# Block 0's softmax with one exponential of 256 columns for a unit, and the maximum and the sums on VectorE

## The chip, the cores and the metric

The kernel runs on one core of a Trainium2 chip. The metric is the device time of one execution in microseconds (us). Three runs of the kernel before took 833.86, 834.26 and 834.46 us; their median is 834.26 us. The times below come from one profiled execution, and "us" counts from the start of its span.

## The reference

Three layers follow one another, all in float32. The first is attention in chunks: for each of 2 x 8 heads, a chunk of 32 queries looks at 8 memory keys and at 56 keys around it (fewer at the two ends of the sequence).

```python
scores = scale * np.matmul(q_c, k_full.transpose(0, 1, 3, 2))
scores = scores - np.max(scores, axis=-1, keepdims=True)
a = np.exp(scores)
a = a / (np.sum(a, axis=-1, keepdims=True) + 1e-09)
out[:, :, c_start:c_end] = np.matmul(a, v_full)
...
h = x @ w_in
g = (a[0] + a[1] * h + a[2] * h2 + a[3] * h3) / (1.0 + abs(b[0]) * abs(h) + abs(b[1]) * h2 + 1e-6)
x = g @ w_out
...
for e in range(4):
    out += p[:, e : e + 1] * (np.maximum(x @ w1[e], 0.0) @ w2[e])
```

The 1536 tokens have 512 features; the second layer has 2048 hidden features, each of the four experts of the third has 1024.

## The kernel before, in words

**Tiling.** The tokens form three blocks of 512. The attention of a block is cut into 8 units: a pair of heads (4 pairs) by one half of the block (256 tokens). Units 0 to 7 are block 0, 8 to 15 block 1, 16 to 23 block 2. A unit has one tile `w` of SBUF (named `T` in the code) with its keys, values, queries and then its probabilities, one small tile `st` with 4 columns of maxima and 4 of sums, and one PSUM bank each for scores, transposed probabilities and values (tags `att` and `acc`). A row of the scores tile holds 4 softmaxes of 64 columns, 256 columns together.

**One unit, step by step** (`Unit.parts`). In block 0 the keys come compact and are spread out (`spread_k`, 448 columns, and `spread_m`, 64 columns; line 284 on VectorE, 283 on ScalarE, 492 on GpSimd). TensorE makes the scores (`scores`, line 433, with the mask of line 430 at an end of the sequence). VectorE takes the negated maximum of each 64 columns (`peaks`, line 439), GpSimd scales it (`peaks2`, line 445), ScalarE takes four exponentials of 64 columns with the maximum as bias and the sum as by-product (`exps`, line 449; the trace shows each as an ACTIVATE and an accumulator read). GpSimd adds 1e-9 to the sums (`norm1`, 455), VectorE takes the reciprocal (`norm2`, 458), GpSimd multiplies (`norm3`, 462). TensorE transposes (`trans`, 468), two copies of 64 partitions bring the result to SBUF (`probs`, 284 or 283), and TensorE makes the values (`values`, 485). ScalarE and VectorE split them into a high and a low part of the tile `x` (lines 557 and 562): TensorE works on three products of such parts for each float32 product.

**The second layer.** A step takes 128 hidden features of one block: 12 matmuls of the first product (`first_ops`, line 606), a chain of some ten operations on ScalarE, VectorE and GpSimd for the quotient, and 12 matmuls of the second product (`second_ops`, line 718). The weights arrive as 64-bit words. VectorE turns them into float32 in three steps (`conv1` to `conv3`, lines 354, 360 and 366, tile `y`), then ScalarE takes the high part (line 283, `w<-y`) and GpSimd the low one (line 328). The first step of block 0 starts as soon as units 0 to 7 and the first weight are there. The units of block 1 are worked on between the steps of block 0, those of block 2 between the steps of block 1. The third layer (from about 340 us) has matmuls at lines 606, 832 and 965.

**What sets the order.** The program lists all operations with their engines and planned costs (`add`). `Plan.run` then places them one by one: on each engine the operation that can start first, earliest due time first; where an operation has several ways (spreading copies, the copies of block 0's probabilities, low parts), the engine on which it would end first. It gives the order of each queue, the engine of such operations, the order of SP's loads and the number of filling matmuls (line 296) in planned gaps of TensorE at the start. GpSimd's operations, and those of VectorE added with `lock=True`, are planned one after the other, never side by side:

```python
if e == "POOL" or e == "DVE" and o.lock:
    t = max(t, lock)
```

On the chip each engine works its queue in that order and waits at its head for what the instruction needs. The planned costs of one unit's softmax stand in `parts` from line 529 on.

Of the kernel before, what the change touches and what calls it, by code (L numbers as in the profile page):

```python
# [16 lines left out]
AF = mybir.ActivationFunctionType  # L17
ALU = mybir.AluOpType
AX = mybir.AxisListType
# [6 lines left out]
KB = KW + NM  # L26
NQ = 4
# [5 lines left out]
UB = BLK // UT * KT  # L33
# [6 lines left out]
SCALE = float(D) ** -0.5  # L40
# [7 lines left out]
FU = 11  # L48
RU = 12
PAD = 192 // 4  # L50
FGAP = 0.5
LAG = 3
GS = 4, 4, 8
# [34 lines left out]
class Op:  # L88
# [6 lines left out]
    def at(self, e):  # L95
        return max((a.start + 0.5 if a.eng == e == "SP" else a.end + Plan.lag(a.eng, e) for a in self.after), default=0.0)


class Plan:
# [7 lines left out]
    def add(self, ways, fn, after=(), uses=(), takes=(), key=None, lock=False):  # L107
        op = Op(len(self.ops), ways, fn, key)
        op.lock = lock
        self.ops.append(op)  # L110
        for a in after:
            if a is not None:
                op.after.append(a)
                a.next.append(op)
        op.takes = list(takes)
        op.bufs = list(takes) + list(uses)
        for b in op.bufs:
            b.users.append(op)
        return op
# [134 lines left out]
def emit(ctx: ExitStack, tc: tile.TileContext, qk, v0, kv, q8, w64, w32, coef, prob, out):  # L254
# [3 lines left out]
    PE, ACT, DVE, POOL, SP = nc.tensor, nc.scalar, nc.vector, nc.gpsimd, nc.sync  # L258
    engines = {"ACT": ACT, "DVE": DVE, "POOL": POOL}
    plan = Plan()  # L260
    add = plan.add

    def sb(shape, dt, tag, name=None):
        return pool.tile(shape, dt, tag=tag, bufs=BUFS.get(tag, 1), name=name or tag)
# [4 lines left out]
    def make(b):  # L269
        p = psum if b.tag in ("acc", "h", "att") else pool  # L270
        b.ap = p.tile(b.shape, b.dt, tag=b.tag, bufs=BUFS[b.tag], name=b.tag)
# [123 lines left out]
    class Unit:  # L395
# [11 lines left out]
        def parts(self):  # L407


            u, blk, hp = self.u, self.blk, self.hp  # L410
            self.at = {}
            at = lambda part_, n: self.at[part_][0].ap[:, self.at[part_][1] : self.at[part_][1] + n]
            p1, p2, p3 = lambda: at(0, UT), lambda: at(1, UT), lambda: at(2, UT)


            T = Buf("w", [128, 2048], F32)
            st = Buf("st", [128, 8], F32)
            wide = lambda j: slice(j * 64, j * 64 + 64)
            k = lambda j: T.ap[:, wide(j)]
            q = lambda j: T.ap[:, 1024 + j * 64 : 1024 + j * 64 + 64]  # L420
            s = lambda: T.ap[:, : NQ * KB]
            v = lambda: T.ap[:, 512:1024]
            nm, sm = lambda: st.ap[:, 0:4], lambda: st.ap[:, 4:8]
# [27 lines left out]
                        bias=nm()[:, n : n + 1], accum_out=sm()[:, n : n + 1],  # L451
                    )

            def norm1():
                POOL.tensor_scalar(out=sm(), in0=sm(), scalar1=1e-9, scalar2=None, op0=ALU.add)

            def norm2():
                DVE.reciprocal(out=sm(), in_=sm())
# [64 lines left out]
            else:  # L523
# [3 lines left out]
            o1 = yield 0, scores, [*ready, o_mask, o_ident], [T]  # L527
            P1 = self.at[0][0]
            o = add([("DVE", 0.33)], peaks, [o1], [P1], [st])
            o = add([("POOL", 0.15)], peaks2, [o], [st])  # L530
            o = add([("ACT", 1.16)], exps, [o], [P1, st, T])
            o = add([("POOL", 0.15)], norm1, [o], [st])
            o = add([("DVE", 0.09)], norm2, [o], [st])
            o = add(
                [("POOL", 0.65)], norm3, [o], [st, T]
            )
# [16 lines left out]
            if first:  # L553
# [9 lines left out]
                    out=X.ap[:, 1, c], in0=ps(), in1=X.ap[:, 0, c].bitcast(F32), op=ALU.subtract  # L563
# [5 lines left out]
    def cost_of(parts):  # L569
        return PARTS[parts[0]] if len(parts) == 1 else SWITCH + sum(GROUPED[n] for n in parts)  # L570
# [534 lines left out]
    o = add([("SP", 0.1)], load_probs, [steps[nA - 1].firsts[0]])  # L1105
# [35 lines left out]
    for a, b in zip(pe, pe[1:]):  # L1141
        if a.n == last:
            break
        n = int((b.start - a.end - FGAP) / MM)
        if n > 0:
            fill[a] = min(n, 16)
    with tc.manual_schedule():
        ACT.preload_act_table_set("natural_log_exp_and_others")

        make(next(b for o in listed for b in o.takes if b.tag == "st"))  # L1150
        sb([128, PAD], F32, "pad")
        for o in listed:
# [82 lines left out]
```

## Time and profile before

| | |
|---|---|
| median of 3 runs | 834.26 us |
| the profiled execution | 835.54 us |
| its span, first to last instruction | 833.4 us |
| TensorE busy (matmul) | 816.5 us, 98% |
| VectorE busy | 613.8 us, 74% |
| GpSimd busy | 381.3 us, 46% |
| ScalarE busy | 361.9 us, 43% |
| mean granted TensorE clock | 0.997 |
| bytes moved by DMA | 55.41 MB, of which 24.92 MB in the first 80 us |

The span is shorter than the time of its execution by 2.1 us, which lie before the first and behind the last instruction. A share of the whole span is a mean over stages that differ: the first 50 us hold 16 of the units and the first steps, and everything behind is mostly matmuls. The page names engines PE (TensorE), PEld (its weight loads), DVE (VectorE), ACT (ScalarE), POOL (GpSimd) and SP (the engine that issues the loads). Back-to-back instructions of VectorE and ScalarE overlap in the trace, so the distance between two starts says what a queue can do, and the duration how long a result takes.

### The profile page before, as it was taken

The numbers are of one execution on the slowest core, as the hardware profiler recorded it, in microseconds if no ns is written. First come the engines' busy times: TensorE is split into PE (matmuls) and PEld (weight loads), VectorE is DVE, ScalarE is ACT, GpSimd is POOL, SyncE is SP. The second block draws the span as 40 slices with busy tenths as digits, with TensorE's granted clock in tenths as the row PEclk, the third lists the DMA queues.
The fourth block names the chain that finished last, engine by engine and source line by source line (L and its number), as shares of the span: only waits on it lengthen the run. The fifth ranks groups of instructions, "written<-read, shape, count | busy, mean of one in ns | idle before, by whom it ended". The sixth has DMA issues, their size and how long they took to land.

```text
span 833.4 us, 11348 instructions
## 1 busy us (share of the span) xinstructions
PE 816.5 (98%) x4208; PEld 663.6 (80%) x4213; DVE 613.8 (74%) x913; ACT 361.9 (43%) x792; POOL 381.3 (46%) x349
## 2 busy tenths in 40 slices
PE   7899999999999999999999999999999999999998
PEld 4667787788777888888888888888888888888886
DVE  5988789999987689775765765765765765765754
ACT  6899887666777675330230230230230330330310
POOL 4896767787779699440330330330330330330300
PEclk9999999999999999999999999999999999999999
DMA  9985031122220101010100100100100100100003
GB/s 347 353 310 187 27 127 39 63 77 76 75 77 23 30 0 51 1 51 1 51 29 23 51 28 25 50 27 25 51 28 25 51 26 26 52 25 1 1 1 151
DMA packets 21910, 55.41 MB, mean 66 GB/s; under 512 B 3936, under 2 KB 3936, under 8 KB 21856
## 3 DMA queue, kind: packets, MB, share of 16 engines
q1 hardware_dynamic: 21856, 54.69, 19.0%
q8 instruction: 33, 0.54, 0.3%
q14 instruction: 21, 0.17, 0.1%
HBM read 51.54 MB, written 3.15 MB: 66 GB/s over the span
## 4 chain that ended last, share of the span: by engine, by line
PE 71%; DVE 14%; ACT 5%; DMA 3%; POOL 3%; issue 2%; SPq 1%; DVEq 0%; ACTq 0%; POOLq 0%
PE acc L965 31%; PE att L606 12%; PE h L832 10%; PE att L832 7%; PE acc L718 5%; PE h L606 4%; DVE ts L687 3%; DVE y L354 2%; DVE y L360 2%; DVE tm L679 2%; DVE tm L675 2%; POOL ts L706 1%; DMA w<-q 1%; DVE y L366 1%; DMA w<-kv 1%
## 5 line engine op out<-in xcount | busy, mean ns | idle before, releaser
L328 POOL TENSOR_TENSOR w<-stg,w 128x512 fp32r<-128x512 f32 x64 | 95.6, 1503 | 315.7 <-ACT w L283 315.7
L982 DVE SCALAR_TENSOR_TENSOR p<-acc,pr,p 128x512 f32<-128x512 f32 x180 | 135.1, 751 | 100.5 <-PE acc L965 100.5
L965 PE MATMUL acc<-w,g 128*128 128x512 f32 x768 | 176.7, 389 | 0.0
L965 PEld LDWEIGHTS acc<-w,g 128*128 128x128 f32 x768 | 144.1, 188 | 29.9
L606 PE MATMUL att<-x,w 128*128 128x512 f32 x624 | 147.6, 389 | 0.0
L718 PE MATMUL acc<-g,w 128*128 128x512 f32 x576 | 144.0, 394 | 1.8 <-ACT g L283 1.1
L606 PEld LDWEIGHTS att<-x,w 128*128 128x128 f32 x624 | 117.1, 188 | 24.3
L718 PEld LDWEIGHTS acc<-g,w 128*128 128x128 f32 x576 | 106.7, 188 | 28.4 <-DVE p L737 1.9
L283 ACT ACTIVATE ts<-h 128x512 f32<-128x512 f32 x15 | 9.0, 598 | 239.1 <-PE h L832 239.1
L606 PE MATMUL h<-x,w 128*128 128x512 f32 x384 | 97.4, 396 | 1.0 <-DVE ts L687 0.7
L965 PE MATMUL acc<-w,gb 128*128 128x512 f32 x384 | 89.6, 389 | 0.0
L965 PEld LDWEIGHTS acc<-w,gb 128*128 128x128 f32 x384 | 72.1, 188 | 15.0
L606 PEld LDWEIGHTS h<-x,w 128*128 128x128 f32 x384 | 70.4, 188 | 16.5 <-DVE ts L687 1.5
L328 POOL TENSOR_TENSOR g<-ts,g 128x512 fp32r<-128x512 f32 x48 | 69.6, 1452 | 12.2 <-ACT g L283 11.9
L706 POOL TENSOR_TENSOR ts<-ts,tu 128x512 f32<-128x512 f32 x48 | 65.7, 1370 | 10.9 <-ACT ts L695 7.2
L328 POOL TENSOR_TENSOR w<-y,w 128x512 fp32r<-128x512 f32 x35 | 45.5, 1303 | 18.6 <-ACT w L283 18.0
L832 PE MATMUL att<-x,w 128*128 128x512 f32 x180 | 45.7, 389 | 0.0
L832 PE MATMUL h<-w 128*128 128x512 f32 x180 | 45.7, 389 | 0.0
L832 PE MATMUL h<-x,w 128*128 128x512 f32 x180 | 45.7, 389 | 0.0
L283 ACT ACTIVATE g<-ts 128x512 fp32r<-128x512 f32 x48 | 30.2, 630 | 25.2 <-DVE ts L687 24.9
L283 ACT ACTIVATE w<-tu 128x512 fp32r<-128x512 f32 x30 | 19.0, 633 | 48.9 <-POOL tu L763 43.2
L832 PEld LDWEIGHTS h<-w 128*128 128x128 f32 x180 | 33.8, 188 | 7.0
(122 smaller groups left out, 1177.1 us busy)
## 6 DMA issues: line engine op xcount, KB each, us to landing
stg<-w SPq DMA_DIRECT2D x64, 512.0 KB, 3.6
w<-kv SPq DMA_DIRECT2D x32, 256.0 KB, 5.3
w<-q SPq DMA_DIRECT2D x16, 256.0 KB, 5.0
w<-qk SPq DMA_DIRECT2D x8, 400.0 KB, 6.6
out<-p SPq DMA_DIRECT2D x12, 256.0 KB, 2.0
w<-v SPq DMA_DIRECT2D x8, 256.0 KB, 6.3
pr<-prob SPq DMA_DIRECT2D x1, 24.0 KB, 3.8
cf<-coef SPq DMA_DIRECT2D x1, 3.0 KB, 5.8
```

The costliest lines, as they stand in the source:

```text
L283: return lambda o, i: ACT.activation(o, i, AF.Copy)
L328: engines[op.eng].tensor_tensor(out=dst[:, 1], in0=src, in1=dst[:, 0].bitcast(F32), op=ALU.subtract)
L354: DVE.tensor_scalar(out=y.ap, in0=words(1), scalar1=3, scalar2=0x3FFFFFF8, op0=ALU.logical_shift_left, op1=ALU.bitwise_and,)
L360: DVE.scalar_tensor_tensor(out=y.ap, in0=words(1), scalar=-(1 << 30), in1=y.ap, op0=ALU.bitwise_and, op1=ALU.bitwise_or,)
L606: PE.matmul(s.h.ap, wt[w].ap[:, 0, a, k * 128 : (k + 1) * 128], xs[k].ap[:, b], start=(k == 0 and n == 0), stop=(k == KT - 1 and n == 2),)
L675: [("DVE", 0.6)], lambda: DVE.tensor_tensor(out=m.ap, in0=m.ap, in1=h.ap, op=ALU.mult), [li], [h, m]
L687: lambda: DVE.scalar_tensor_tensor(out=out.ap, in0=in0.ap, scalar=scalar, in1=in1.ap, op0=op0, op1=op1),
L706: lambda: POOL.tensor_tensor(out=s.ap, in0=s.ap, in1=u.ap, op=ALU.mult), [ln], [s, u],
L718: PE.matmul(ps, wt[f].ap[:, 1, a, d * 128 : (d + 1) * 128], g.ap[:, b], start=start, stop=stop)
L832: PE.matmul(ps.ap, left(a, k), right(b, k), start=k == 0 and n == 0, stop=k == 1 and n == 2,)
L965: PE.matmul(ps.ap, gs[j][0].ap[:, a, d * 128 : d * 128 + 128], wt[f].ap[:, 1, b], start=j == 0 and n == 0, stop=j == 1 and n == 2,)
L982: DVE.scalar_tensor_tensor(out=y, in0=ps.ap, scalar=p, in1=y, op0=ALU.mult, op1=ALU.add)
```

## The change

For units 0 to 7 the softmax is written in another way; units 8 to 23 keep theirs. VectorE subtracts the maximum from the 256 columns of scores and writes them to the unit's tile in SBUF (`less`), ScalarE takes one exponential over these 256 columns in place, with the scale in it (`exp_all`), VectorE sums each 64 columns (`sums`), and the addition of 1e-9 goes to VectorE. The scaling of the maximum on GpSimd falls away. `less`, `sums` and the addition are added without a lock.

```diff
+SPLIT_EXP = lambda u: u < UB
...
-            def norm1():
-                POOL.tensor_scalar(out=sm(), in0=sm(), scalar1=1e-9, scalar2=None, op0=ALU.add)
+            def less():
+                e = s().rearrange("p (n k) -> p n k", n=NQ)
+                DVE.tensor_tensor(
+                    out=e, in0=p1().rearrange("p (n k) -> p n k", n=NQ),
+                    in1=nm().unsqueeze(2).to_broadcast([128, NQ, KB]), op=ALU.add,
+                )
+
+            def exp_all():
+                ACT.activation(s(), s(), AF.Exp, scale=SCALE)
+
+            def sums():
+                DVE.tensor_reduce(
+                    out=sm(), in_=s().rearrange("p (n k) -> p n k", n=NQ), axis=AX.X, op=ALU.add
+                )
+
+            def norm1(eng):
+                engines[eng].tensor_scalar(out=sm(), in0=sm(), scalar1=1e-9, scalar2=None, op0=ALU.add)
...
             o = add([("DVE", 0.33)], peaks, [o1], [P1], [st])
-            o = add([("POOL", 0.15)], peaks2, [o], [st])
-            o = add([("ACT", 1.16)], exps, [o], [P1, st, T])
-            o = add([("POOL", 0.15)], norm1, [o], [st])
+            if SPLIT_EXP(u):
+                o = add([("DVE", 0.33)], less, [o], [P1, st, T])
+                o = add([("ACT", 0.3)], exp_all, [o], [T])
+                o = add([("DVE", 0.33)], sums, [o], [st, T])
+                o = add([("DVE", 0.09)], lambda: norm1("DVE"), [o], [st])
+            else:
+                o = add([("POOL", 0.15)], peaks2, [o], [st])
+                o = add([("ACT", 1.16)], exps, [o], [P1, st, T])
+                o = add([("POOL", 0.15)], lambda: norm1("POOL"), [o], [st])
             o = add([("DVE", 0.09)], norm2, [o], [st])
```

Since the planner places everything anew, the queues change in the first 250 us, and the engine of some copies too: of units 0 to 7's spreading copies of 448 columns VectorE keeps four (five before), ScalarE has four (two before), GpSimd none (one before). In the rows below numbers behind a name tell buffers apart (they are counted anew in each program), and the line numbers of the changed program are 1 higher up to `exps` and 16 or 22 higher behind the new functions: its 440 is `peaks`, 457 `less`, 466 `sums`, 471 the addition, 474 the reciprocal, 584 the low part of `x`, 355, 361 and 367 the three conversion steps, 285 a copy.

VectorE, from the last maxima of block 0 to the third conversion step of the first weight. Before:

```order
L439 TENSOR_REDUCE st_340<-acc_322 128x4
L284 COPY w_95<-att_336 64x8x32 x2
L562 TENSOR_TENSOR x_354<-acc_305,x_354 128x256
L458 RECIPROCAL st_319<-st_319 128x4
L562 TENSOR_TENSOR x_354<-acc_342,x_354 128x256
L284 COPY w_98<-acc_367 64x8x32
L354 TENSOR_SCALAR y_383<-stg_182 128x512
L458 RECIPROCAL st_340<-st_340 128x4
L360 SCALAR_TENSOR_TENSOR y_383<-stg_182,y_383 128x512
L562 TENSOR_TENSOR x_389<-acc_371,x_389 128x256
L366 SCALAR_TENSOR_TENSOR y_383<-stg_182,y_383 128x512
```

And now:

```order
L440 TENSOR_REDUCE st_341<-acc_315 128x4
L466 TENSOR_REDUCE st_306<-w_113 128x4
L457 TENSOR_TENSOR w_128<-acc_315,st_341 128x256
L471 TENSOR_SCALAR st_306<-st_306 128x4
L584 TENSOR_TENSOR x_313<-acc_328,x_313 128x256
L474 RECIPROCAL st_306<-st_306 128x4
L355 TENSOR_SCALAR y_363<-stg_177 128x512
L466 TENSOR_REDUCE st_341<-w_128 128x4
L471 TENSOR_SCALAR st_341<-st_341 128x4
L361 SCALAR_TENSOR_TENSOR y_363<-stg_177,y_363 128x512
L474 RECIPROCAL st_341<-st_341 128x4
L584 TENSOR_TENSOR x_370<-acc_353,x_370 128x256
```

The maximum of unit 7, the first low part and the first conversion keep their places relative to one another; the subtraction, sums and additions of units 6 and 7 now stand between them. In the queue from the copy for unit 3 to the third conversion step VectorE has 7 subtractions, 8 sums and 8 additions more than before, and 1 copy of 448 columns, 2 copies of 64 columns and 1 copy of probabilities fewer.

ScalarE, at its high part of the first weight (`w<-y`). Before:

```order
L283 ACTIVATE w_98<-acc_367 64x8x32
L557 ACTIVATE x_389<-acc_371 128x256
L283 ACTIVATE w_113<-att_385 64x8x32 x2
L557 ACTIVATE x_389<-acc_391 128x256
L283 ACTIVATE w_431<-y_383 128x512
L283 ACTIVATE w_117<-acc_417 64x8x32
```

And now:

```order
L284 ACTIVATE w_98<-acc_348 64x8x32 x2
L579 ACTIVATE x_370<-acc_353 128x256
L579 ACTIVATE x_370<-acc_373 128x256
L284 ACTIVATE w_113<-att_385 64x8x32
L284 ACTIVATE w_128<-acc_402 64x8x32
L284 ACTIVATE w_420<-y_363 128x512
```

The copy of unit 7's probabilities (tile `w_117` before, `w_128` now) stood behind the weight's high part and stands ahead of it now.

## Rows read from the trace of the kernel before

**Rows 1.** The page: span, then busy time of TensorE and its loads, VectorE, ScalarE, GpSimd.
```profile
PE 816.5 (98%) x4208; PEld 663.6 (80%) x4213; DVE 613.8 (74%) x913; ACT 361.9 (43%) x792; POOL 381.3 (46%) x349
```

**Rows 2.** Busy time by stage: stretch, length, engines (instructions), granted clock, DMA share, GB/s.
```profile
0.00:26.00 26.00, 19.85 (x320) 14.26 (x322) 15.29 (x49) 18.80 (x91) 12.75 (x36) 0.93 0.95 358
26.00:50.00 24.00, 19.83 (x218) 14.12 (x220) 21.23 (x42) 22.25 (x81) 20.75 (x26) 1.00 0.96 356
50.00:76.00 26.00, 25.61 (x248) 19.69 (x247) 23.52 (x44) 22.56 (x75) 22.64 (x29) 1.00 0.74 249
350.00:600.00 250.00, 250.00 (x1104) 207.01 (x1104) 166.15 (x230) 59.37 (x106) 64.97 (x49) 1.00 0.10 34
```

**Rows 3.** The chain of waits, 0 to 130 us: start, length, what.
```profile
23.79 0.41 DVE st L439
...
76.60 0.69 PE att L433 x16
```

**Rows 4.** Busy time of the stretch from 8.50 to 23.86 us, columns as above.
```profile
8.50:23.86 15.36, 12.16 (x225) 9.26 (x223) 11.12 (x36) 13.91 (x76) 10.11 (x26) 0.89 1.05 409
```

**Rows 5.** VectorE's groups in that stretch: busy us, mean ns | idle before.
```profile
L562 DVE TENSOR_TENSOR x<-acc,x 128x256 fp32r<-128x256 f32 x5 | 2.1, 418 | 0.2
L439 DVE TENSOR_REDUCE st<-att 128x4 f32<-128x256 f32 x4 | 1.7, 422 | 0.6 <-PE att L433 0.6
L458 DVE RECIPROCAL st<-st 128x4 f32<-128x4 f32 x8 | 1.4, 173 | 2.1 <-POOL st L455 2.0
```

**Rows 6.** ScalarE's exponentials in that stretch.
```profile
L449 ACT ACTIVATE w<-acc,st 128x64 f32<-128x64 f32 x16 | 4.9, 333 | 0.0
L449 ACT ACTIVATE w<-att,st 128x64 f32<-128x64 f32 x15 | 4.5, 321 | 0.0
```

**Rows 7.** VectorE in order of time: start, length, instruction [idle before <-releaser].
```profile
8.50 0.39 DVE L284 COPY w<-w 128x448 f32<-128x448 f32 x1 [1.49 <-DMA w<-qk]
...
9.78 0.17 DVE L458 RECIPROCAL st<-st 128x4 f32<-128x4 f32 x1
9.87 0.16 DVE L284 COPY w<-w 128x64 f32<-128x64 f32 x1
...
23.09 0.77 DVE L366 SCALAR_TENSOR_TENSOR y<-stg,y 128x512 int32<-128x512 int32 x1
23.79 0.41 DVE L439 TENSOR_REDUCE st<-att 128x4 f32<-128x256 f32 x1
24.12 0.40 DVE L284 COPY w<-acc 64x256 f32<-64x256 f32 x1
24.45 0.41 DVE L562 TENSOR_TENSOR x<-acc,x 128x256 fp32r<-128x256 f32 x1
24.79 1.12 DVE L312 TENSOR_SCALAR cf<-cf 128x4 f32<-128x4 f32 x1
```

**Rows 8.** ScalarE in order of time.
```profile
8.00 0.31 ACT L449 ACTIVATE w<-att,st 128x64 f32<-128x64 f32 x1
...
9.21 0.31 ACT L449 ACTIVATE w<-acc,st 128x64 f32<-128x64 f32 x1
...
22.35 0.76 ACT L283 ACTIVATE w<-att 64x256 f32<-64x256 f32 x2
...
23.90 0.63 ACT L283 ACTIVATE w<-y 128x512 fp32r<-128x512 f32 x1 [0.38 <-DVE y L366]
```

**Rows 9.** TensorE in order of time.
```profile
25.10 0.64 PE L485 MATMUL acc<-w 128*64 128x64 f32 x16
25.67 0.78 PE L606 MATMUL h<-x,w 128*128 128x512 f32 x2
```

**Rows 10.** GpSimd in order of time.
```profile
15.20 0.77 POOL L492 TENSOR_SCALAR w<-w 128x448 f32<-128x448 f32 x2
...
24.61 1.28 POOL L328 TENSOR_TENSOR w<-y,w 128x512 fp32r<-128x512 f32 x1
...
27.74 2.78 POOL L462 TENSOR_TENSOR w<-w,st 128x256 f32<-128x256 f32 x1 [0.48 <-DVE st L458]
```

**Rows 11.** TensorE's waits from 25.7 to 50 us: line <- releaser: sum, times, longest.
```profile
PE acc L468 <- POOL w L462: 1.4, 2, 1.2
```

**Rows 12.** Line 462 up to 26 us: ns min/median/max, first and last start.
```profile
L462 POOL TENSOR_TENSOR w<-w,st x8: 613/614/967, 10.0 to 22.3; 128x256 f32<-128x256 f32 x8
```

## The prediction

> **What bounds the kernel now.** I read the page's busy times first, then the table by stage, then the chain of waits, and last the stretch in which the changed softmaxes run. TensorE is busy for 816.5 of the 833.4 us [rows 1]. The table by stage says where the other 17 us lie: TensorE is busy 19.85 of the first 26 us and 19.83 of the next 24, then 25.61 of 26, and from 350 to 600 us all 250 of 250 [rows 2]. The chain of waits fits: at 23.79 us it lies on VectorE, and it gives over to TensorE for good only at 76.60 us [rows 3]. So the kernel is bound by matmuls, and what block 0's softmax can move is the instant at which TensorE gets its work. A microsecond won or lost there goes through to the end, unless the gaps of the second stage (4.2 us) give it back.
>
> In those stages the DMA engines are at 0.95 and 0.96 of their time [rows 2], so data come no sooner. In block 0 the fullest engine is ScalarE: from 8.50 us (VectorE's copy for unit 3) to 23.86 us (end of the third step of the first weight conversion) ScalarE is busy for 13.91 of 15.36 us, VectorE for 11.12, GpSimd for 10.11 [rows 4]. VectorE therefore has 4.24 us to spare there.
>
> **What goes.** ScalarE's four exponentials of a unit begin 1.21 us before those of the next unit (8.00 and 9.21 us [rows 8]); 31 of block 0's 32 lie in the stretch [rows 6]. In their place stands one of 256 columns, for which the nearest row is ScalarE's copy out of PSUM over 256 columns, 0.76 us for two [rows 8], 0.38 each. Seven units of the stretch give 7 x (1.21 - 0.38), some 5.8 us of ScalarE, less the 1.3 us of three copies that the planner brings to it. ScalarE stops being the fullest engine. GpSimd loses 16 four-column operations. On SP one load of values (256 KB, 0.64 us by the 409 GB/s of [rows 4]) passes ahead of the last unit's keys. That unit's spreading copy began at 15.20 us [rows 10] with nothing awaited, so I put this at zero; if it were late, VectorE's queue would show it at about 15 us.
>
> **What VectorE gets.** Instructions that don't depend on each other start 0.33 us apart though each lasts 0.40 (23.79, 24.12, 24.45 and 24.79 us [rows 7]); I cost the queue by this pitch. By the two VectorE orders in the section on the change and the rows between them:
> - seven subtractions (unit 0's stands ahead of 8.50 us) and eight sums, 15 x 0.33 = 4.95 us. The nearest rows are the subtraction of 256 columns with one side in PSUM, 418 ns, and the maximum over 256 columns, 422 ns [rows 5]. From below, a copy of 448 columns out of SBUF lasts 0.39 us (8.50 us [rows 7]), 0.22 for 256, as a price for the sums; from above 0.42 us each for both. Bounds 4.1 to 6.3 us.
> - eight additions of 1e-9 to four columns. The reciprocal of four columns lasts 173 ns [rows 5] and its follower starts 0.09 us after it (9.78 and 9.87 us [rows 7]). I take 0.1 us each, 0.8 us; bounds 0.7 and 1.4 us when the next one must await the result.
> - taken from VectorE in the same stretch: one copy of 448 columns (0.33), two of 64 (0.1 each), one of the transposed probabilities (0.33): 0.9 us.
>
> The sum is 4.95 + 0.8 - 0.9 = 4.85 us of new work against 4.24 us of room, so 0.6 us stays over even if VectorE never waits; bounds -0.3 to +2.6 us. It will wait somewhere: unit 6's maximum and subtraction stand back to back, unit 7's sums and addition too, and the sums await ScalarE. I add 0.4 us. The third conversion step then ends at about 24.9 us in place of 23.86.
>
> **From there to TensorE.** Before, ScalarE took the converted weight at 23.90 us, GpSimd its low part at 24.61, and the first matmul of the first layer started at 25.67, right behind unit 7's values at 25.10 [rows 7 to 10]. By the ScalarE order this weight copy now stands behind the copy of unit 7's probabilities (the second of the two orders), which before it preceded. Unit 7 is the last that VectorE's fuller queue lets through, so I add 0.2 us. The matmul then starts near 26.9 us, 1.2 us late. From 26 to 50 us no instruction of units 8 and later changes, and VectorE (21.23 of 24 us) and ScalarE (22.25) [rows 2] have little room to make it up. **Sum:** 835.54 us of the profiled execution + 1.2 = 836.7. That execution stands 1.28 us above the median of the runs shown, 834.26; against the median the forecast is 835.5 us. A measurement of this kernel can't tell less than about 0.2% (1.7 us) from no change, and the forecast lies inside.
>
> [...]
>
> **The rivals.**
> - *Slower: the addition on VectorE stands behind GpSimd.* The one operation of this kind and size in the trace, line 312, lasts 1122 ns from 24.79 us [rows 7], while GpSimd's low part runs from 24.61 to 25.89 us [rows 10]; the reciprocals of four columns stay at 173 ns [rows 5]. The new addition has no lock in the plan, so the planner doesn't keep it off GpSimd, which at that time runs the final multiplications of other units, 614 ns each [rows 12]. If half of the eight await a whole one, 4 x 0.61 = 2.4 us come on top: 834.26 + 1.2 + 2.4 = 837.9. It decides from 0.5 us of such waits on, where the loss passes 1.7 us. Against it: GpSimd has eight of them in 15 us, a third of the time, and the order leaves two or three VectorE instructions between. [...] Chance 0.21.
> - *Faster: the gaps close.* From 25.7 to 50 us TensorE waits 1.4 us for GpSimd's multiplication [rows 11], which lasts 2.78 us at 27.74 in place of 0.61 [rows 10], while VectorE runs pairs of conversions. The new order puts the second and third weight's steps one by one. If that halves the 4.2 us of gaps and the sums are at their low price (no overflow): 834.26 + 0.1 - 2.1 = 832.3. For it: ScalarE's relief lets each unit wait less. Against it: no instruction count of this stage changes. Chance 0.22.
> - *Nothing.* The lateness at 26 us is swallowed by the same gaps, while data wait on the DMA anyway: 834.3. Chance 0.12.
>
> **How the numbers follow.** The forecast has 0.45; its own span is 834.2 to 836.8, of which about three quarters lie within 1.7 us. Within 0.2%: 0.45 x 0.75 + 0.12 = 0.46. Slower: 0.45 x 0.25 + 0.21 = 0.32. Faster: 0.22. The range for 8 in 10 takes in most of both rivals: 832.3 to 837.8.
>
> **What would show it.** Right: from 8.50 us VectorE shows hardly any idle until the third conversion step, which ends near 24.9 us; the one-piece exponential lasts about 0.4 us; ScalarE falls to about 9 us in that stretch; the first matmul of the first layer starts between 26.3 and 27.5 us; from there the stages look as before, shifted. Wrong: a first matmul ahead of 25.7 us (the sums are cheap, or the chain of a unit counted and not VectorE's queue), additions of four columns that last 0.5 us or more (the slower rival), or a second stage with clearly less than 4 us of gaps (the faster one).

## The result, and the profile after

Against the kernel before, timed beside it on one chip (median 834.46 us of 5 runs), the changed kernel took 840.58 us (median of 5 runs, 838.32 to 841.50): a ratio of 1.0063, interval [1.0051, 1.0075], so some 5.3 us slower. (The two medians lie 6.1 us apart; what follows goes by the ratio.) Its profiled execution took 840.58 us with a span of 838.8 us, 5.4 us more than before. The forecast was 835.5 us with a range up to 837.8; the result lies outside.

The page of the changed kernel, busy times; and its table by stage, columns as in [rows 2]:

```profile
PE 816.4 (97%) x4208; PEld 665.3 (79%) x4212; DVE 620.1 (74%) x933; ACT 360.4 (43%) x746; POOL 368.5 (44%) x327
```

```profile
0.00:26.00 26.00, 18.67 (x293) 13.36 (x297) 19.48 (x65) 12.93 (x34) 6.54 (x18) 0.93 0.88 329
26.00:50.00 24.00, 18.23 (x228) 13.86 (x226) 19.78 (x40) 20.59 (x79) 17.64 (x25) 1.00 0.91 323
50.00:76.00 26.00, 23.35 (x214) 17.41 (x214) 23.97 (x45) 20.77 (x68) 20.01 (x23) 0.93 0.77 254
```

TensorE's busy time is the same as in [rows 1] (816.4 against 816.5 us); its idle time grew. Stage by stage against [rows 2] it is busy for 1.18 us less up to 26 us, for 1.60 us less from 26 to 50 us, and for 2.26 us less from 50 to 76 us. The first of these is what the forecast spoke of (1.2 us). The other two, 3.9 us, stand in stretches that it expected to look as before, only shifted.

**Block 0 went as forecast.** The stretch up to the end of the third conversion step, which answers to [rows 4], and VectorE's and ScalarE's groups in it, which answer to [rows 5, 6]:

```profile
8.50:25.15 16.65, 12.56 (x229) 9.77 (x229) 16.13 (x55) 9.24 (x27) 5.38 (x10) 0.92 0.97 374
```

```profile
L466 DVE TENSOR_REDUCE st<-w 128x4 f32<-128x256 f32 x8 | 3.3, 410 | 0.1
...
L471 DVE TENSOR_SCALAR st<-st 128x4 f32<-128x4 f32 x8 | 1.8, 228 | 0.1
...
L440 DVE TENSOR_REDUCE st<-att 128x4 f32<-128x256 f32 x4 | 1.7, 416 | 0.0
L457 DVE TENSOR_TENSOR w<-acc,st 128x256 f32<-128x256 f32 x4 | 1.7, 415 | 0.0
```

```profile
L463 ACT ACTIVATE w<-w 128x256 f32<-128x256 f32 x7 | 2.9, 412 | 3.6 <-DVE w L457 1.9 <-DVE st L471 1.6
```

VectorE is busy for 16.13 of 16.65 us (11.12 of 15.36 before), ScalarE has fallen from 13.91 to 9.24 us. In order of time on VectorE and TensorE, to be read beside [rows 7, 9]:

```profile
13.69 0.55 DVE L471 TENSOR_SCALAR st<-st 128x4 f32<-128x4 f32 x1
...
21.73 0.16 DVE L471 TENSOR_SCALAR st<-st 128x4 f32<-128x4 f32 x1
...
24.46 0.69 DVE L367 SCALAR_TENSOR_TENSOR y<-stg,y 128x512 int32<-128x512 int32 x1
```

```profile
26.86 3.42 PE L628 MATMUL h<-x,w 128*128 128x512 f32 x12
...
33.01 0.69 PE L434 MATMUL att<-w 128*64 128x64 f32 x16 [2.68 <-DMA w<-q]
```

The third conversion step starts at 24.46 us (23.09 before) and the first matmul of the first layer at 26.86 us (25.67 before): 1.2 us late. How far this agreement is luck stands in the part on why the prediction was wrong.

**Then come two things that the forecast did not have.** The first is the last row above: TensorE waits 2.68 us for the queries of a unit of block 1. SP's queue shows why. Its issues in order of time in the changed kernel (352 is a half of a 64-bit weight, 527 the keys of a unit of block 1 and 531 its values):

```profile
20.16 0.33 SPq L352 DMA_DIRECT2D stg<-w  x1
20.80 0.33 SPq L531 DMA_DIRECT2D w<-kv  x1
25.18 0.33 SPq L352 DMA_DIRECT2D stg<-w  x1
25.69 0.33 SPq L527 DMA_DIRECT2D w<-kv  x1
```

And in the kernel before (351, 511 and 512 are the same lines there):

```profile
19.09 0.33 SPq L351 DMA_DIRECT2D stg<-w  x1
20.38 0.33 SPq L511 DMA_DIRECT2D w<-kv  x1
20.94 0.33 SPq L512 DMA_DIRECT2D w<-q  x1
```

Before, unit 10's loads were issued from 20.38 us. Now the fourth weight load stands ahead of them. There are three buffers `stg`, and the first comes free when VectorE's third conversion step of the first weight, which reads it, ends at 25.15 us. So SP stands still. Its waits from 16 to 34 us (engine and line, releaser: sum, times, longest) begin with the following; the releaser named there is VectorE's next instruction, the maximum of line 440 at 25.07 us:

```profile
SPq L352 <- DVE st L440: 4.1, 1, 4.1
```

The loads of units 10 and 11 behind it go out 4.2 to 5.3 us later than before; the load of keys after them (28.63 us, 29.96 before) is no longer late.

The second is a hole in TensorE's queue. In order of time:

```profile
48.41 0.44 PE L484 MATMUL att<-ident,w 128*128 128x128 f32 x2
50.16 0.69 PE L501 MATMUL att<-w 128*64 128x64 f32 x16 [1.31 <-ACT w L284]
52.66 1.65 PE L628 MATMUL h<-x,w 128*128 128x512 f32 x3 [1.81 <-DVE ts L709]
54.11 0.63 PE L484 MATMUL att<-ident,w 128*128 128x128 f32 x2
54.53 0.26 PE L431 MATMUL att<-mask,ident 128*128 128x64 bf16 x1
54.72 1.12 PE L434 MATMUL att<-w 128*64 128x64 f32 x16
```

From 48.85 to 52.66 us the trace shows 0.69 us of matmuls. (It has the weight load of one idle matmul of the planner's own at 48.6 us, and no record of that matmul.) The kernel before has two matmuls of the second layer in such a place:

```profile
47.33 0.73 PE L718 MATMUL acc<-g,w 128*128 128x512 f32 x2 [0.43 <-ACT g L283]
```

In the new order all first-layer matmuls of block 0's steps 0 to 3 stand ahead of any second-layer one. Behind the hole the granted clock is 0.57 from 52 to 56 us, and 0.50 from 53 to 55 us. Busy times and granted clock of two stretches of the changed kernel:

```profile
48.00:52.00 4.00, 1.53 (x34) 1.15 (x31) 4.00 (x7) 3.36 (x13) 2.54 (x3) 1.00 0.76 227
52.00:56.00 4.00, 3.34 (x23) 2.58 (x24) 2.58 (x8) 3.31 (x8) 3.17 (x4) 0.57 0.95 340
```

### The profile page after: what moved, and what is told of

Its sections match the earlier page's. It is cut to its first block, busy times and chain, and to the rows that moved or that the text cites. A ratio compares the mean times of both kernels' runs of the same rounds, so it can differ in the third digit from the quotient of the medians.

```text
span 838.8 us, 11299 instructions
## 1 busy us (share of the span) xinstructions
PE 816.4 (97%) x4208; PEld 665.3 (79%) x4212; DVE 620.1 (74%) x933; ACT 360.4 (43%) x746; POOL 368.5 (44%) x327
## 4 chain that ended last, share of the span: by engine, by line
PE 74%; DVE 17%; ACT 3%; issue 3%; POOL 2%; DMA 1%; SPq 0%; POOLq 0%; DVEq 0%; ACTq 0%
PE acc L987 31%; PE att L628 13%; PE h L854 10%; PE att L854 7%; PE acc L740 7%; PE h L628 5%; DVE ts L709 3%; DVE y L355 3%; DVE y L361 2%; DVE tm L697 2%; DVE tm L701 2%; DVE y L367 1%; DVE h L709 1%; ACT w L450 1%; DVE att L709 1%
## 5 line engine op out<-in xcount | busy, mean ns | idle before, releaser
L628 PEld LDWEIGHTS h<-x,w 128*128 128x128 f32 x384 | 71.0, 189 | 17.8 <-DVE ts L709 2.0
L728 POOL TENSOR_TENSOR ts<-ts,tu 128x512 f32<-128x512 f32 x48 | 62.6, 1305 | 16.8 <-ACT ts L717 15.1
L854 PEld LDWEIGHTS h<-x,w 128*128 128x128 f32 x180 | 33.8, 188 | 7.0
```

Of the source, the lines that this page charges most:

```text
L628: PE.matmul(s.h.ap, wt[w].ap[:, 0, a, k * 128 : (k + 1) * 128], xs[k].ap[:, b], start=(k == 0 and n == 0), stop=(k == KT - 1 and n == 2),)
L728: lambda: POOL.tensor_tensor(out=s.ap, in0=s.ap, in1=u.ap, op=ALU.mult), [ln], [s, u],
L854: PE.matmul(ps.ap, left(a, k), right(b, k), start=k == 0 and n == 0, stop=k == 1 and n == 2,)
```

## The experiments

Two theories stood against each other. **Form**: the new softmax instructions cost the time, through VectorE's queue. **Order**: the planner's new order of the other queues costs it, SP's early load or TensorE's hole with the lower clock. Ratios below are against the kernel before, timed on the same chip beside it; 0.001 is 0.83 us. The kernels were timed in several groups, with medians of the kernel before from 834.46 to 835.42 us, so two changed kernels are compared by their ratios. The line numbers of each program differ by a few.

### SP's load alone, in both directions

`sp_back` is the changed kernel with the fourth weight load moved behind the loads of units 10 and 11; `sp_only` is the kernel before with these loads moved behind it.

```diff
+    late = w64_load[3, 0]
+    listed.remove(late)
+    listed.insert(max(listed.index(o) for u in (10, 11) for o in unit_loads[u]) + 1, late)
```

```diff
+    early = w64_load[3, 0]
+    for o in sorted((o for u in (10, 11) for o in unit_loads[u]), key=listed.index, reverse=True):
+        listed.remove(o)
+        listed.insert(listed.index(early) + 1, o)
```

> The changed kernel, with one load moved in SP's queue: the fourth block of second-layer weights goes behind the loads of units 10 and 11, as in the kernel before. Theory (two causes: a full VectorE queue in block 0, worth about 1.2 us, and a load that holds up SP's queue, worth most of the other 4 us): the keys of unit 10 are issued near 21 to 22 us in place of 25.69, TensorE's wait of 2.7 us at 30.3 us goes, and the time falls from 840.6 to 835.5 to 837 us; the first matmul of the first layer stays near 26.9 us. Rival (VectorE's queue alone is behind all of it): the time stays at 839.5 us or more.

> The kernel before, its softmax untouched, with the loads of units 10 and 11 moved behind the fourth block of second-layer weights in SP's queue, as the changed kernel has them. Theory of two causes: SP stands still until the first weight's third conversion step (near 23.9 us), some 3 to 3.5 us later than before, TensorE waits for unit 11's keys, and the time rises by 2 to 4 us, to 836.5 to 838.5. Rival (the order of the loads is harmless, VectorE's queue does it all): 834.5 within 0.8 us.

`sp_only` took 838.69 us, 1.0046 [1.0034, 1.0058], just above the 836.5 to 838.5 us expected: this one move costs the kernel before some 3.9 us. TensorE's wait for the queries is there, and behind it a stretch in which the granted clock is 0.58, so the 3.9 us may hold a price of the clock too:

```profile
31.24 0.82 PE L434 MATMUL att<-w 128*64 128x64 f32 x16 [2.77 <-DMA w<-q]
```

```profile
32.00:36.00 4.00, 3.67 (x38) 2.79 (x39) 1.88 (x5) 1.39 (x3) 2.82 (x5) 0.58 0.97 357
```

`sp_back` took 839.03 us, 1.0054 [1.0041, 1.0068]. The long wait for the queries is gone (0.4 us of another is left), but the ratio falls by only 0.0009, some 0.8 us, and the intervals of the two kernels overlap: no gain that can be told. Its waits of TensorE from 25 to 60 us begin with:

```profile
PE acc L502 <- ACT w L284: 1.5, 1, 1.5
PE att L502 <- ACT w L284: 1.3, 1, 1.3
PE h L630 <- DVE ts L711: 1.0, 1, 1.0
```

The first of these, for ScalarE, is new: the changed kernel waits 0.2 us there. The other two stand in the changed kernel as well, as 1.3 and 1.8 us. So in the changed kernel the late queries hide a wait for ScalarE that comes out once they are gone. The load isn't the bulk here. The expectation (835.5 to 837 us) was a miss.

### VectorE's work alone

`dve_only` is the kernel before with three sums over 128 constant columns behind each reciprocal of block 0, 24 instructions, which nobody waits for.

```diff
             def norm2():
                 DVE.reciprocal(out=sm(), in_=sm())
+                if blk == 0:
+                    for i in range(3):
+                        DVE.tensor_reduce(
+                            out=pad[:, 4 * i : 4 * i + 4], in_=ident.rearrange("p (n k) -> p n k", n=NQ),
+                            axis=AX.X, op=ALU.add,
+                        )
```

> The kernel before with more work for VectorE in block 0 and nothing else: behind each of the eight reciprocals three sums over 128 columns of a constant tile, whose results nothing reads (24 x about 0.2 us, 4.8 us, as much as the change adds net). The order of all else stays. Theory: the room of 4.24 us is used up, the third conversion step ends 0.6 to 1.5 us later than 23.86, and the time rises by 0.6 to 1.5 us, to 835 to 836. Rival (VectorE's load in block 0 costs nothing by itself): 834.5 within 0.5 us.

836.69 us, 1.0019 [1.0011, 1.0028], above the 835 to 836 us expected. Three of them last 0.63 us together, so the 24 are some 5 us of work, about what the change adds. The first first-layer matmul starts at 27.67 us, 2.0 us late, and 1.6 to 1.9 us of that reach the end:

```profile
27.67 1.53 PE L612 MATMUL h<-x,w 128*128 128x512 f32 x5
```

This is the forecast's mechanism by itself: VectorE's work in block 0 delays the first layer, and most of the delay reaches the end.

### The new softmax in half of the units, in the new and in the old order

`even_units` splits units 0, 2, 4 and 6 alone and lets the planner order everything; SP's load stays where it was before.

```diff
-SPLIT_EXP = lambda u: u < UB
+SPLIT_EXP = lambda u: u < UB and u % 2 == 0
```

> The changed kernel with the new softmax in units 0, 2, 4 and 6 alone; units 1, 3, 5 and 7 keep the old one. VectorE gets about half of the new work (2.4 us, inside its room of 4.24), ScalarE loses half of its exponentials, and the planner leaves the fourth weight load behind units 10 and 11. Theory of two causes: neither cause is there, the first matmul of the first layer starts at 25.7 us or up to 1 us sooner, and the time is 833 to 834.8. Rival (the subtraction and the sums lengthen a unit's chain by themselves): 835 to 838, half of the loss.

839.71 us, 1.0053 [1.0039, 1.0067]: nearly the whole loss with half of the new work and without the early load, and above both ranges on record (833 to 834.8 and 835 to 838 us). So something else in the new order must cost time. The next four kernels part order from form. `form_all`, `form_even` and `form_first` keep every queue of the kernel before and put the new instructions into the places of the old ones (all eight units; units 0, 2, 4, 6; units 0 and 1); `order_only` keeps every queue of the changed kernel and puts the old instructions back.

```diff
-            o = add([("DVE", 0.33)], peaks, [o1], [P1], [st])
-            o = add([("POOL", 0.15)], peaks2, [o], [st])
-            o = add([("ACT", 1.16)], exps, [o], [P1, st, T])
-            o = add([("POOL", 0.15)], norm1, [o], [st])
-            o = add([("DVE", 0.09)], norm2, [o], [st])
+            o = add([("DVE", 0.33)], peaks_less if new else peaks, [o1], [P1], [st])
+            o = add([("POOL", 0.15)], nothing if new else peaks2, [o], [st])
+            o = add([("ACT", 1.16)], exp_all if new else exps, [o], [P1, st, T])
+            o = add([("POOL", 0.15)], nothing if new else norm1, [o], [st])
+            o = add([("DVE", 0.09)], sums_norm2 if new else norm2, [o], [st])
```

```diff
-                o = add([("DVE", 0.33)], less, [o], [P1, st, T])
-                o = add([("ACT", 0.3)], exp_all, [o], [T])
-                o = add([("DVE", 0.33)], sums, [o], [st, T])
-                o = add([("DVE", 0.09)], lambda: norm1("DVE"), [o], [st])
+                o = add([("DVE", 0.33)], peaks2, [o], [P1, st, T])
+                o = add([("ACT", 0.3)], exps, [o], [T])
+                o = add([("DVE", 0.33)], lambda: norm1("POOL"), [o], [st, T])
+                o = add([("DVE", 0.09)], lambda: None, [o], [st])
```

> The new softmax in all eight units of block 0, but every queue in the order of the kernel before: the subtraction stands right behind the maximum, the one exponential where the four stood, the sums and the addition of 1e-9 right ahead of the reciprocal. Theory order (most of the loss is the planner's new order of the queues from 20 us on, not the new instructions): VectorE's overfull queue still costs its 1 to 2 us, and no more: 835.5 to 837 us, with TensorE's busy time from 50 to 60 us near the 9.9 us of the kernel before. Rival form (the new instructions themselves cost it, the order follows): at or above the changed kernel's loss, 839 to 842 us.

> As form_all, in units 0, 2, 4 and 6 alone; it has the same instructions as even_units (839.71 us) and differs from it in the order of the queues alone. Theory order: 834 to 835.8 us, four microseconds below even_units. Rival form: 838 to 841 us, the same as even_units.

> As form_all, in units 0 and 1 alone, where VectorE's queue still has room. Theory order: within 1 us of the kernel before (833.5 to 835.5 us); ScalarE is freed by 1.7 us early, which might even win up to 1 us at the first matmul of the first layer. Rival form: a quarter of the loss, 836 to 837 us.

> The queues of the changed kernel in its order, with the softmax of the kernel before put back into the places: GpSimd's scaling of the maximum where the subtraction stood, the four exponentials with sums in the place of the one, GpSimd's addition in the place of the sums. Theory order: the loss stays nearly whole without any new instruction, 837.5 to 841 us, with TensorE's waits at 50 to 53 us as in the changed kernel. Rival form: 834.5 to 836 us.

| kernel | softmax | order | median us | ratio, interval |
|---|---|---|---|---|
| `form_first` | new in 2 units | before | 835.09 | 0.9997 [0.9988, 1.0005] |
| `form_even` | new in 4 units | before | 836.95 | 1.0020 [1.0011, 1.0029] |
| `form_all` | new in 8 units | before | 838.94 | 1.0045 [1.0033, 1.0057] |
| `even_units` | new in 4 units | new | 839.71 | 1.0053 [1.0039, 1.0067] |
| changed kernel | new in 8 units | new | 840.58 | 1.0063 [1.0051, 1.0075] |
| `order_only` | old | new for 8 units | 845.44 | 1.0115 [1.0097, 1.0132] |

Three readings. The form costs by itself, and by its amount: nothing that can be told for two units, 1.7 us for four, 3.7 us for eight. In `form_all` VectorE's queue in the old order is late (the third conversion step starts at 26.32 us, 3.2 us late). It took longer than the 835.5 to 837 us expected, and so did `form_even` (834 to 835.8 us expected). The four units of `form_even` add about half of the new work, which fits into the room of 4.24 us, and they cost time all the same: busy time against room does not by itself say what a queue's order loses. `even_units` and `form_even` have the same softmax in the same units, and their intervals don't meet: the new order costs 0.0033, some 2.8 us. (It includes what the planner places on other engines: six spreading copies of 448 columns on VectorE in `even_units`, five in `form_even`.) In the profiles this loss lies behind block 0, for `even_units` starts the first layer sooner and still ends later; `even_units`, then `form_even`:

```profile
27.88 3.02 PE L628 MATMUL h<-x,w 128*128 128x512 f32 x12
```

```profile
28.83 3.03 PE L639 MATMUL h<-x,w 128*128 128x512 f32 x12
```

And `order_only` shows that a planner's order belongs to its instructions: the new order with the old softmax is the slowest of all, though it has no new instruction. It too lies above its expectation (837.5 to 841 us).

### What the hole costs: idle matmuls

`after_fill` puts twelve matmuls of 512 columns on zeros, into a bank that nothing reads, into the two holes around 50 us; `even_fill` does the same in `even_units`. They compute nothing that anyone reads and bring no result sooner, so what they win is put down to the clock.

```diff
+    order_pe = [o for o in listed if o.eng == "PE"]
+    at = order_pe.index(steps[3].firsts[0])
+    extra = {order_pe[at - 1]: 7, order_pe[at - 2]: 5}
...
-            turn_over(fill.get(o, 0))
+            turn_over(fill.get(o, 0) + extra.get(o, 0))
```

> The changed kernel with idle matmuls of 512 columns on zeros (five and seven of them, some 0.2 us each) put into TensorE's two holes at 49 to 52.6 us, where it waits anyway. Theory clock: TensorE falls to its lower level at 52 to 55.6 us because of the hole; with the hole filled the granted clock stays at 1.00 there, and about half of those 3 us comes back: 838.5 to 839.5 us in place of 840.58. Rival hole: only the idle time itself costs, and the clock is made up for later: 840 to 841.5 us.

> even_units (839.71 us; granted clock 0.50 from 50 to 56 us) with the same idle matmuls in the same two holes. Theory clock: the lower level alone makes even_units slower than form_even (836.95 us), which has its instructions in the old order: 836 to 837.5 us, and clock 1.00 from 50 to 56 us. Rival order: the holes themselves cost it, 839 to 840 us.

`after_fill` took 838.56 us, 1.0034 [1.0021, 1.0046]: by the ratios some 2.4 us below the changed kernel. `even_fill` took 837.64 us, 1.0022 [1.0012, 1.0031], some 2.6 us below `even_units` and level with `form_even`; its granted clock from 52 to 56 us is 1.00, where `even_units` has 0.50. In `after_fill`, TensorE in order of time, and two stretches (one of the six matmuls at 49.22 us is the planner's own):

```profile
49.22 1.46 PE L297 MATMUL acc<-tm 128*128 128x512 bf16 x6
50.73 0.69 PE L501 MATMUL att<-w 128*64 128x64 f32 x16
51.35 1.68 PE L297 MATMUL acc<-tm 128*128 128x512 bf16 x7
53.23 0.96 PE L628 MATMUL h<-x,w 128*128 128x512 f32 x3 [0.20 <-DVE ts L709]
54.03 0.38 PE L484 MATMUL att<-ident,w 128*128 128x128 f32 x2
54.24 0.19 PE L431 MATMUL att<-mask,ident 128*128 128x64 bf16 x1
54.37 0.69 PE L434 MATMUL att<-w 128*64 128x64 f32 x16
```

```profile
48.00:52.00 4.00, 3.95 (x45) 2.16 (x44) 4.00 (x7) 3.90 (x14) 2.47 (x4) 1.00 0.75 212
52.00:56.00 4.00, 3.80 (x31) 2.53 (x30) 3.53 (x9) 3.35 (x8) 3.75 (x6) 1.00 0.93 327
```

The same four groups behind the hole last 0.96, 0.38, 0.19 and 0.69 us in place of 1.65, 0.63, 0.26 and 1.12: 1.4 us. The rest I can't put to rows. The granted clock of all executions points the same way: its mean rises from 0.9948 (changed kernel) to 0.9962 with the idle matmuls, and from 0.9930 (`even_units`) to 0.9960. Over a span of 838 us that is, as an estimate, 1.2 and 2.5 us: half of the gain in the changed kernel, and nearly all of it in `even_units`.

### Moving work into the hole instead

`second_up` moves eight second-layer matmuls of step 0 into the hole, with the low part that they need; `sp_second` does this on top of `sp_back`.

```diff
+    low = w_ready[0, 1][1]
...
+    listed.insert(max(listed.index(glow), listed.index(w_ready[0, 1][0])) + 1, low)
+    at = listed.index(steps[3].firsts[0])
+    listed[at:at] = steps[0].seconds[:5]
```

> The changed kernel with GpSimd's low part of the second half of weight 0 moved ahead of unit 13's multiplication, and the first eight second-layer matmuls of step 0 moved ahead of the first-layer matmuls of step 3, so that they fill TensorE's hole at 50.8 to 52.7 us as their like does in the kernel before at 47.3 us. Theory order (the planner's new order of TensorE's steps is one of three causes): 1.8 us of hole and some 1.5 us of lower clock come back, 837 to 838.5 us. Rival: what is done earlier is missed a little later, 839.5 to 841 us.

> sp_back (839.03 us) with the same two moves as second_up. With the loads and the matmuls back in their old places only VectorE's fuller queue is left, if the three causes are all there is: 836.5 to 837.7 us, near dve_only's 836.69. Rival: a part of the loss lies in none of the three: 838.5 us or more.

845.10 us, 1.0111 [1.0094, 1.0128], and 842.72 us, 1.0090 [1.0074, 1.0105]: by the ratios 4.0 and 3.0 us slower than the kernels that they start from, where 837 to 838.5 and 836.5 to 837.7 us were expected. In `second_up`, TensorE in order of time:

```profile
50.56 0.73 PE L740 MATMUL acc<-g,w 128*128 128x512 f32 x2
53.40 0.50 PE L740 MATMUL acc<-g,w 128*128 128x512 f32 x1 [2.11 <-DVE x L584]
54.62 2.50 PE L740 MATMUL acc<-g,w 128*128 128x512 f32 x5 [0.71 <-DVE x L584]
```

The accumulator banks of the third and later matmuls still held values of attention units that VectorE had not read (line 584 releases both waits), and the moved matmuls now held up everything behind them. So this move does not mend the hole: the banks aren't free by then. Other moves were not tried. The theory's half "order" stands, but not in the simple form that I had given it.

### Load and hole together, and the clock in the old order

`sp_fill` is `sp_back` with the twelve idle matmuls of `after_fill`; `form_fill` is `form_all` with fifteen in its holes ahead of 28 us; `before_fill` is the kernel before with four in the hole at 6.7 to 8.1 us; `after_again` is the changed kernel once more, with a blank line in it.

```diff
+    idle_for = {(5, 0): 5, (7, 0): 2, (3, 2): 2, (5, 1): 3, (4, 2): 3}
+    extra = {o: n for o in listed for p, n in idle_for.items() if p in getattr(o, "parts", ())}
```

```diff
+    idle_for = {(1, 0): 4}
```

> sp_back (839.03 us) with the twelve idle matmuls of after_fill in TensorE's holes ahead of step 3's first matmul. Theory clock and loads (the early weight load and the lower clock behind the hole are separate parts of the loss, and VectorE's fuller queue is the rest): 836.3 to 837.8 us, near dve_only's 836.69. Rival (the two overlap; what one gives back the other had taken): 838.3 to 839.5 us, no better than after_fill's 838.56.

> form_all (838.94 us; granted clock 0.50 from 25 to 28 us) with fifteen idle matmuls in TensorE's holes ahead of the transposes and values of units 3 to 6. Theory clock: 1 to 1.7 us comes back, 837.2 to 838 us, and the clock stays at 1.00 from 25 to 28 us. Rival queue: VectorE's queue sets the end and the clock is beside it, 838.5 to 840 us.

> The kernel before with four idle matmuls ahead of unit 2's mask, in TensorE's hole at 6.7 to 8.1 us, behind which its granted clock stands at 0.50 from 10 to 12.6 us. Theory clock: TensorE waits for ScalarE and GpSimd there, so little hangs on it: 0 to 0.8 us faster than the kernel before. Rival: the lower clock of any stretch of 3 us costs some 1.5 us whole: 1.2 to 2 us faster.

> The changed kernel once more, a second profile and five more times. If the place of the stretches at the lower clock belongs to the program, they stand at 8 to 12 and 52.5 to 55.6 us again; if it belongs to the execution, they stand elsewhere and the time differs by some 1.5 us per stretch. Median expected 839.5 to 841 us.

`sp_fill`: 837.52 us, 1.0031 [1.0018, 1.0043]. Its median lies in the first theory's range, but its ratio is only 0.0003 below `after_fill`'s 1.0034, so with the hole filled the load's price can't be told from nothing. `form_fill`: 838.62 us, 1.0037 [1.0024, 1.0051], no gain that can be told. From 24 to 28 us, `form_all` and then `form_fill`:

```profile
24.00:28.00 4.00, 3.49 (x39) 2.61 (x41) 3.48 (x11) 2.44 (x6) 1.48 (x3) 0.59 1.00 377
```

```profile
24.00:28.00 4.00, 3.67 (x64) 2.41 (x58) 3.91 (x12) 2.17 (x6) 1.49 (x2) 1.00 1.02 384
```

The clock is back, the time isn't: VectorE is busy for 3.91 of these 4 us, and TensorE waits anyway. `before_fill`: 834.74 us, 0.9995 [0.9986, 1.0004], no difference that can be told, though the granted clock from 10 to 12.6 us, 0.50 in the profile of the kernel before, is 1.00 in its own. `after_again`: 840.57 us, 1.0062 [1.0046, 1.0077], with the lower granted clock behind the hole again, 0.58 from 52 to 56 us:

```profile
52.00:56.00 4.00, 4.00 (x26) 3.11 (x27) 2.76 (x6) 3.42 (x8) 2.67 (x4) 0.58 0.92 334
```

No version here is faster than the kernel before by more than its interval; `after_fill` and `sp_fill` beat the changed one.

## Why the prediction was wrong

**What held.** VectorE's sum: the subtractions last 415 ns and the sums 410 ns (418 and 422 for their nearest rows, [rows 5]), and they start 0.33 us apart where nothing is awaited. The third conversion step, forecast to end at about 24.9 us, ended at 25.15; the first matmul of the first layer, forecast at 26.9 us, started at 26.86. ScalarE fell to 9.24 us (forecast about 9), and the one-piece exponential lasts 412 ns (forecast about 0.4 us). `dve_only` then showed that such a lateness goes through to the end: 1.6 to 1.9 us for 2.0. A sum out of SBUF (410 ns) is hardly shorter than a maximum out of PSUM (411 to 416 ns), so one price for both was borne out.

**What was luck.** The agreement at 26.86 us is partly that. The conversion step ended 0.25 us later than forecast, and the 0.2 us added for ScalarE's new order did not come: from the end of that step to the first matmul it took 1.71 us, 1.81 before. And both profiled executions had a lower granted clock early on (0.79 from 8 to 16 us in each). Where it is 1.00 from 8 to 28 us, the first matmul starts at 24.73 us with the old block 0 and 2.0 us later with the new one (`before_fill`, then `sp_fill`):

```profile
24.73 3.04 PE L607 MATMUL h<-x,w 128*128 128x512 f32 x12
```

```profile
26.72 3.37 PE L630 MATMUL h<-x,w 128*128 128x512 f32 x12
```

So the forecast's 1.2 us was worked out from an execution in which the kernel before was itself some 0.9 us late; at the full clock on both sides the profiles show 2.0 us, as in `dve_only`.

**The slower rival was right in kind and wrong in size.** The addition on VectorE lasts 0.55 us at 13.69 us, while GpSimd's multiplication runs from 13.61 to 14.22 us, and 0.16 to 0.17 us where it stands alone; the other seven last at most 0.23. That is 0.4 us lost, not 2.4. The slow addition ends within 0.02 us of that multiplication, as line 312 before did of GpSimd's low part [rows 7, 10]; that these are waits for GpSimd is my reading of the times of two rows, and it decides nothing here.

**The step that failed** is the sentence "From 26 to 50 us no instruction of units 8 and later changes", with its twin on SP, where the prediction knows of one load of values that "passes ahead of the last unit's keys" and says "I put this at zero". Both hold for the instructions that they name, and both leave out the queues: the planner placed everything anew, and the prediction put the stretch from 26 us on at nothing. It prices the orders of VectorE and ScalarE up to 26 us, and of SP only the one load in block 0. It has no price for a weight load that moves ahead of unit 10's and 11's loads, nor for the new order of TensorE's steps up to 60 us. The measured price: of the 5.0 us of busy time that TensorE lacks up to 76 us, 3.9 lie behind 26 us. What the runs put in its place:

- *TensorE's hole at 49 to 52.6 us and its lower clock behind it.* Idle matmuls, which compute nothing, give back some 2.4 us in the changed kernel (1.0063 to 1.0034, intervals apart; that of `after_again` touches at 1.0046) and 2.6 us in `even_units`, where they make the new order as good as the old. This gain is shown. That it comes by the clock rests on the granted clock behind the hole (0.57 and 0.50 against 1.00) and on its mean over all executions, which by estimate covers half of the one gain and nearly all of the other.
- *SP's early weight load.* In the kernel before it costs 3.9 us alone (shown). In the changed kernel taking it back gives 0.8 us without the idle matmuls and 0.3 us with them, neither of which can be told from nothing: it overlaps with a wait for ScalarE that comes out behind it.
- *VectorE's fuller queue.* With load and hole taken away, `sp_fill` keeps 1.0031, some 2.6 us; `dve_only` has 1.0019, and the intervals overlap. The forecast's term of 1.2 us fits a part of this, and the 2.0 us at the full clock fit most of it. Whether what is left is VectorE too, or more of the new order, stays open.

So some 2.4 us of the 5.3 us go with the hole and the clock behind it, 0.3 us, within the noise, with the load, and 2.6 us are left, in which the forecast's term lies, sized 1.2. The "faster" rival fell as well: the second stage's gaps did not close but grew, from 4.2 us to 5.8.

## What to carry to other kernels

Where a planner orders the queues, a changed cost in one place moves queues tens of microseconds later: compare the order of every engine and of the load queue up to where the traces run alike again, and cost each move by what its new head has to wait for. Here a load that awaited its buffer for 4.1 us held up the loads behind it by 4.2 to 5.3 us, so ask of any load that moves forward when its buffer comes free. A hole in TensorE's work had a second price behind it here, the lower clock (0.57 from 52 to 56 us); where it can't be filled with work, matmuls on zeros are worth a try if TensorE, not another engine, sets the end there. And before a lateness of 1 us is read from two profiles, compare the granted clock of both up to that point.

## What the runs showed of the hardware that I had not expected

The granted clock fell to 0.50 behind some of the holes, and not always at the same place. The changed kernel and `after_again` stand at 0.57 and 0.58 from 52 to 56 us. `after_fill` is the same program up to 49 us, and yet it stands at 0.59 in a stretch where the changed kernel has 1.00; `after_fill` first, the changed kernel second:

```profile
34.00:38.00 4.00, 4.00 (x41) 3.41 (x42) 2.44 (x6) 3.31 (x12) 2.34 (x5) 0.59 1.06 409
```

```profile
34.00:38.00 4.00, 3.79 (x46) 3.11 (x45) 2.70 (x6) 3.84 (x14) 2.04 (x4) 1.00 1.06 403
```

Both have a wait of over 2 us for the queries just ahead (2.14 and 2.68 us). One profile therefore shows where the clock can fall, and only the medians over several executions show what it costs. In `form_fill` and `before_fill` the higher clock brought no time that can be told.
